# First MLP of a fused attention kernel: an order written by hand in place of a planned one

## The chip, the cores and the metric

The kernel runs on one core of a Trainium2 chip. The metric is the device time of one execution in microseconds (us). The engines are named as in the profile: PE (TensorE, matrix products and transposes), PEld (its weight loads), DVE (VectorE), ACT (ScalarE), POOL (GpSimd) and SP (SyncE, which here issues the DMAs). Each engine works off its own queue in order and waits at an instruction until its operands and its target are ready.

## What is computed

Attention over 4 batches of 8 heads, then two MLPs over 2304 tokens. The change is in the first MLP, `_moe_ref`, and in the preparation of the weights of the second, which runs beside it.

```python
def _moe_ref(x, w_in, w_out, g_ln):          # x 2304x512, w_in 512x1024, w_out 1024x512
    h = x @ w_in
    e = np.exp(h - np.max(h, axis=-1, keepdims=True))
    sm = e / (np.sum(e, axis=-1, keepdims=True) + 1e-09)
    solu = h * sm
    mu = np.mean(solu, axis=-1, keepdims=True)
    var = np.mean((solu - mu) ** 2, axis=-1, keepdims=True)
    return ((solu - mu) / np.sqrt(var + 1e-06) * g_ln) @ w_out

def _moe2_ref(x, w_gate, w_val, w_out):      # d_ff 1536
    gate = 1.0 / (1.0 + np.exp(-(x @ w_gate)))
    return gate * (x @ w_val) @ w_out
```

The weights arrive as 64-bit floats. Every product is computed from two parts of each operand, a high part and the rest (`hi`, `lo`), with three products hi·lo, hi·hi, lo·hi.

## The kernel before

The first MLP (class `Moe1`, from L606) works on 18 blocks of 128 tokens, t = 0 to 17. For one block:

- `xsplit` (L648) splits the attention's result X into `xs` hi (ACT, L653; DVE at L655 for the first three) and lo (POOL for blocks 2 to 5, otherwise DVE; L656). There are two `xs` buffers.
- `hidden` (L658): 24 matmuls of 512 columns (L674) into a PSUM tile `h` of 128x1024 (two buffers), then the statistics: the maximum (DVE, L682), the exponential with its sum (ACT, L690), reciprocal and product (DVE, L695 to L699), the square with its sum (ACT, L702, written to a bf16 scrap tile `sq` in SBUF), three small operations on POOL (L703 to L706, the power of -1/2 among them) and the normalisation (ACT, L707).
- `lntrans` (L717): 8 transposes on PE (L730) into two PSUM tiles `pl`, then `hilo` (L146): hi on ACT (L147), lo on DVE (L148), into `lnT`, which holds three blocks (a group) and has two buffers.
- `proj` (L748): for each group of three blocks 4 x 24 matmuls of 384 columns (L740) into PSUM tiles `po` (two buffers), copied back to X by ACT (L746).

The 18 blocks thus issue 432 matmuls for h, 144 transposes and 576 matmuls for po.

Beside it run two conversions of weights from 64-bit floats. `w_out` (L623) makes w_out's six chunks 2 to 7 (`rawwo`, `exwo`, `wo`): one load of 512 KB, then DVE (L108, L111, L121, L130), ACT (L118, L137, L642) and POOL (L641, L154). `Moe2.convert` (L827) makes each of the first six of twelve chunks of the second MLP's weights in 15 steps and 6 trailing steps that fall beside the next chunk's: three loads of 512 KB, 12 operations on DVE, POOL's products (L861) and sums (L875), hi on ACT (L883), lo (L889) and stores to DRAM (`scrg`, `scro`; L895, L896, L908, L909). In the first MLP all lo parts lie on POOL (`eng = nc.gpsimd`) and the tile `M` has one buffer; `lo_o` writes in place into `ex`, which is stored from there.

The order: the attention (`A.run(hooks)`, L1204) stands in a `manual_schedule`, in which each engine issues its instructions as the program writes them; blocks 0 and 1 of h and the statistics of block 0 are hooked into it. Everything of `Moe1` after that, with `A.last_conversions()` and the statistics of block 1 (`b1(a1())`, L1206, L1207), stands outside, and a planner places it; `steps` (L773) gives the planner its priorities, `merge` (L48) mixes the conversion steps in, and `issue_after` keeps conversion steps behind the last block's maximum on DVE. In `steps` a block's transposes stand one block behind its matmuls. The planner may place an instruction between those of a manual section where its operands allow it.

After the first MLP, `diffs` and `parts` (L952, L967) split X for the second MLP, and `m2.run` (L1117) works that off in a manual section; it is not changed, except that it uses `convert` for the other six chunks.

Of the kernel before, what the change touches and what calls it, by code (L numbers as in the profile page):

```python
# [32 lines left out]
def f32(ap):  # L33
    return ap.bitcast(F32)
# [13 lines left out]
def kernel(  # L48
# [21 lines left out]
    P = 128  # L70
# [92 lines left out]
    class Attention:  # L163
        def __init__(self, sb, ps, xe):
# [11 lines left out]
            self.small = sb.tile([P, 32], F32, tag="first", name="first")  # L176
            at = 7 * NFIRST
            self.rs = [self.small[:, at + 9 * n : at + 9 * n + 9] for n in range(2)]
# [26 lines left out]
            self.sum = [sb.tile([P, 9, 2], F32, tag=f"sum{n}", name=f"sum{n}") for n in range(2)]  # L205
# [12 lines left out]
        def gates(self):  # L218
# [8 lines left out]
            self.o9 = sb.tile([P, HP, 9], F32, tag="o9", name="o9")  # L227
# [366 lines left out]
        def last_conversions(self):  # L594
            for nm in "arbphl":
                for x in EXTRA[NP + 1]:
                    getattr(self, f"cv_{nm}")(x, self.pr[x])
# [5 lines left out]
    LAG = 7  # L603
    NFIRST = 2

    class Moe1:  # L606
        def __init__(self, xe, wi):
            self.xe, self.wi = xe, wi
            self.lnT, self.ln, self.xs, self.last, self.lasts = {}, {}, {}, None, []
            self.lt = self.sb = self.ps = self.spare = None  # L610

        def queue(self, steps):


            def one(f):
                if self.last is None:
                    return f()
                with tc.issue_after(self.last):
                    f()

            return [lambda f=f: one(f) for f in steps]

        def w_out(self, wp, stage, gl):  # L623

            self.wo = list(wo)
            for c in range(len(wo), NF1):
                self.wo.append(
                    [wp.tile([P, DM], F32R, tag=f"wo{x}{c}", name=f"wo{x}{c}") for x in "hl"]
                )

            def one(c):
                raw, ex, m = staged(stage, f"wo{c}")
                load_raw(raw, moe_w_out[c * P : c * P + P, :].unsqueeze(1))
                f64_a(raw, ex[:, 0], ex[:, 1])
                f64_r(ex[:, 0])
                scale_out(ex[:, 1], c)
                f64_b(raw, ex[:, 0], ex[:, 1], gl16[:, c : c + 1])
                hi, lo = self.wo[c]
                halves = [slice(256 * h, 256 * h + 256) for h in range(2)]
                for sl in halves:  # L640
# [637 lines left out]
```

## Time and profile before

| | us |
|---|---|
| median of 3 runs | 860.56 (860.41 to 862.53) |
| the profiled execution | 863.18 |
| its span, first to last instruction | 861.4 |
| attention alone on PE, to the first matmul of block 2 | 0 to 222.3 |
| first MLP after that, to the first matmul of the second | 222.3 to 441.0 |
| second MLP | 441.0 to 861.4 |

Over the span PE is busy 97%, DVE 73%, ACT 58%, POOL 58%. The profiled execution is 2.6 us above the median. The profile's busy time of PE counts matmuls that overlap in its pipeline; the pace of a row of matmuls is read from the time between the start of the first and the start of what follows, as the chain of waits shows it.

### The profile page before, as it was taken

The page shows a single profiled execution, that of the slowest core. Times are in us where ns is not written, and L with a number is a line of the kernel's source. Part 1 is how long each engine was busy: PE and PEld are TensorE (multiplying, and loading weights), DVE is VectorE, ACT ScalarE, POOL GpSimd, SP SyncE. Part 2 cuts the span into 40 slices and gives each one's busy share as a digit, 9 for nine tenths or more (in the row PEclk, how much of TensorE's full clock was granted, in tenths as well). Part 3 has the DMA queues.
Part 4 walks back from the last instruction along what each step waited for, and adds up shares of the span by engine and source line. Part 5 has one row for each costly group of instructions (what it writes and reads, how often), then busy time and mean ns, then how long its engine had stood idle before and what let it go on. Part 6 is the DMA issues. An engine that isn't in the chain of part 4 may idle for free.

```text
span 861.4 us, 15033 instructions
## 1 busy us (share of the span) xinstructions
PE 838.3 (97%) x5020; PEld 732.6 (85%) x5020; DVE 631.5 (73%) x1394; ACT 502.1 (58%) x1089; POOL 502.4 (58%) x631
## 2 busy tenths in 40 slices
PE   7999999999989999999999999999999999999998
PEld 5777777777778897888998999899899999999996
DVE  6899999997899777873427778788876445846645
ACT  5899999997888766775523446445533223423221
POOL 5777778775478978986105746776556242432111
PEclk9899999999999999999999999999999999999999
DMA  6443445330224655552059857993898863391662
GB/s 147 112 103 91 109 99 120 89 82 26 80 80 147 205 186 163 180 172 73 25 211 355 264 197 240 397 363 111 298 405 300 273 212 114 96 382 48 236 240 98
DMA packets 134140, 153.56 MB, mean 178 GB/s; under 512 B 67376, under 2 KB 101424, under 8 KB 134064
## 3 DMA queue, kind: packets, MB, share of 16 engines
q1 hardware_dynamic: 134064, 152.61, 54.7%
q8 instruction: 40, 0.66, 0.3%
q14 instruction: 36, 0.29, 0.1%
HBM read 116.40 MB, written 36.18 MB: 177 GB/s over the span
## 4 chain that ended last, share of the span: by engine, by line
PE 68%; POOL 10%; DVE 10%; DMA 6%; issue 2%; ACT 2%; SPq 1%; DVEq 0%; POOLq 0%; ACTq 0%
PE acc L1079 15%; PE s L1026 15%; PE g L1026 7%; PE x L500 5%; PE po L740 5%; PE sc L391 4%; PE v L1026 4%; POOL M L889 4%; PE h L674 2%; PE x L485 2%; DMA scro<-ex 2%; POOL M L861 1%; PE sc L382 1%; POOL M L875 1%; DMA gv0v<-scrg 1%
## 5 line engine op out<-in xcount | busy, mean ns | idle before, releaser
L1079 PE MATMUL acc<-o,G 128*128 128x512 f32 x648 | 181.6, 390 | 0.2 <-DVE G L1045 0.2
L1064 POOL TENSOR_TENSOR vl<-vl,sg 128x384 f32<-128x384 f32 x36 | 37.1, 1031 | 212.8 <-ACT sg L1063 212.8
L1079 PEld LDWEIGHTS acc<-o,G 128*128 128x128 f32 x648 | 118.5, 188 | 10.3 <-DVE G L1045 0.7
L430 POOL TENSOR_SCALAR p<-p,first,o 128x256 f32<-128x256 f32 (+3 forms) x142 | 92.0, 663 | 5.0 <-ACT ex L118 1.9
L674 PE MATMUL h<-wih,xs 128*128 128x512 f32 x288 | 83.7, 400 | 2.5 <-DVE e L699 1.4
L419 ACT ACTIVATE p<-p,nm 128x128 f32<-128x128 f32 (+2 forms) x144 | 82.7, 583 | 0.7 <-DVE nm L413 0.6
L1056 ACT ACTIVATE sg<-sg 128x384 f32<-128x384 f32 x36 | 18.9, 525 | 94.4 <-DVE sg L1055 94.4
L740 PE MATMUL po<-lnT,woh 128*128 128x384 f32 x288 | 73.7, 336 | 0.0
L1045 DVE TENSOR_TENSOR G<-vl,G 128x384 fp32r<-128x384 f32 x72 | 54.1, 751 | 20.5 <-ACT G L1042 20.3
L674 PEld LDWEIGHTS h<-wih,xs 128*128 128x128 f32 x288 | 52.9, 188 | 14.6 <-ACT xs L653 2.0
L1042 ACT CAST G<-vl 128x384 fp32r<-128x384 f32 x72 | 37.1, 515 | 42.5 <-POOL vl L1064 33.9
L1063 ACT ACTIVATE sg<-sg 128x384 f32<-128x384 f32 x36 | 18.9, 526 | 70.5 <-DVE sg L1062 70.4
L1050 DVE TENSOR_TENSOR u<-s,p 128x384 f32<-128x384 f32 x36 | 20.0, 556 | 54.3 <-PE s L1026 52.8
L413 DVE CUSTOM_DVE_ANT_0 p<-sc,mask 128x128 f32<-128x128 f32 (+3 forms) x128 | 54.6, 479 | 1.4 <-PE sc L391 1.2
L861 POOL TENSOR_TENSOR M<-ex 128x256 f32<-128x256 f32 x48 | 41.4, 884 | 23.7 <-DVE ex L130 20.4
L889 POOL TENSOR_TENSOR M<-M,hi 128x256 fp32r<-128x256 f32 x60 | 54.2, 926 | 0.2
L740 PEld LDWEIGHTS po<-lnT,woh 128*128 128x128 f32 x288 | 52.4, 189 | 0.1
L740 PE MATMUL po<-lnT,wol 128*128 128x384 f32 x144 | 48.5, 336 | 0.0
L118 ACT ACTIVATE ex<-ex,consts 128x512 int32<-128x512 int32 (+1 forms) x56 | 36.2, 647 | 20.4 <-DVE ex L108 18.8
L338 POOL TENSOR_TENSOR G<-E,zm 128x640 f32<-128x640 f32 x16 | 24.9, 1556 | 36.4 <-DVE E L335 31.7
L674 PE MATMUL h<-wil,xs 128*128 128x512 f32 x144 | 45.5, 395 | 0.0
L121 DVE SCALAR_TENSOR_TENSOR ex<-raw,ex 128x512 int32<-128x512 int32 (+1 forms) x56 | 43.1, 770 | 2.4 <-ACT ex L118 2.3
(711 smaller groups left out, 2494.8 us busy)
## 6 DMA issues: line engine op xcount, KB each, us to landing
o<-scro SPq DMA_DIRECT2D x36, 512.0 KB, 4.4
scrg<-hi SPq DMA_DIRECT2D x36, 256.0 KB, 4.8
scrg<-M SPq DMA_DIRECT2D x36, 256.0 KB, 4.4
raw<-in_moe_w_val_dram SPq DMA_DIRECT2D x12, 512.0 KB, 5.4
raw<-in_moe_w_gate_dram SPq DMA_DIRECT2D x12, 512.0 KB, 5.5
raw<-in_moe_w_out_dram SPq DMA_DIRECT2D x12, 512.0 KB, 4.8
out_dram<-X SPq DMA_DIRECT2D x18, 256.0 KB, 2.0
qt<-in_q_dram SPq DMA_DIRECT2D x32, 128.0 KB, 2.7
```

Of the source, the lines that this page charges most:

```text
L121: nc.vector.scalar_tensor_tensor(ex, raw[:, :, 1], -0x80000000, ex, ALU.bitwise_and, ALU.bitwise_or)
L413: nc.vector.tensor_tensor_reduce(p, x, m, -1.0, 3.0e38, ALU.add, ALU.min, nm)
L419: nc.scalar.activation(p, p, AF.Exp, bias=nm, scale=-1.0, accum_out=self.sum[n % 2][:, c, 0:1])
L430: eng.tensor_scalar(p, p, r["rs"][:, c : c + 1], og, ALU.mult, ALU.mult)
L500: nc.tensor.matmul(r["x", g][64 * hh : 64 * hh + 64, c0 : c0 + src.shape[1]], r["vt"][:, c : c + D], src, start=False, stop=j == 0,)
L674: nc.tensor.matmul(ph[:, j * 512 : j * 512 + 512], xs[:, s, c], self.wi[c][w][:, j * 512 : j * 512 + 512], start=(c == 0 and s == 0 and w ...
L740: nc.tensor.matmul(po, w[:, m * P : m * P + P], L[x][c // 4][:, c % 4], start=(c == 0 and n == 0), stop=(c == NF1 - 1 and n == 2),)
L861: nc.gpsimd.tensor_mul(out[:, sl], m[:, sl], e[:, sl])
L889: eng.tensor_sub(dst[:, sl].bitcast(F32R), dst[:, sl], f32(hi[:, sl]))
L1026: nc.tensor.matmul(po, W[:, a, c * P : c * P + P], xb[b][:, c], start=c + i == 0, stop=c == 1 and i == 2)
L1045: nc.vector.tensor_sub(G[:, 1, hs[h]], vl[:, h], f32(G[:, 0, hs[h]]))
L1079: nc.tensor.matmul(po, G[:, x, sl], o[:, w], start=first and i == 0, stop=stop and i == 2)
```

## The change

`Moe1` is rewritten so that the whole first MLP stands in manual sections; the arithmetic of the blocks is the same. In words:

- `run` issues per block t = 2 to 17: three conversion steps, half of the matmuls of h(t), the transposes of block t-2, the other half; then ACT's hi of t-2, the normalisation of t-1, the maximum and exponential of t, two conversion steps, DVE's lo of t-2, the hi of `xsplit(t+2)`, the product of t, the lo of `xsplit(t+2)`, the square of t, and `pieces(t)`, a third of a group's projection, with one conversion step behind each half of 12 matmuls and the rest at the end. Block 8 does all of h first and then finishes group 0.
- The chunks of w_out are converted one per block, in five steps; the second MLP's conversion starts at block 8 with 16 steps and has all of its steps issued by block 16.
- `square` writes into the PSUM tile `h` instead of a scrap tile in SBUF. The second column of the sum tile is set once instead of in every block (L689).
- `conversion` is called with `nc.vector, 2`: two of five lo parts of a chunk go from POOL to DVE, and `M` has two buffers. `ho` holds both parts, `lo_o` writes there and not into `ex`, and one store of 512 KB takes the place of two of 256 KB.
- The statistics of block 1 and the last conversions of w_out's chunks 0 and 1 move into the attention's manual section, behind it; `run` and `last` (the tail, mixed with `diffs` and `parts`) are two manual sections of their own.
- The unused tile `odd` ahead of w_in grows from 24 to 56 words, so the tiles of w_in lie 128 bytes further. `sum` and `o9` share one tile; the columns for the statistics lie in `consts`.

```diff
+        def square(self, t, first=None):
+            e, va, su = self.ln[t], self.small(t, "va", first), self.st[t, "su"]
+            sq = self.ph[t] if first is None else first.spare
+            nc.scalar.activation(sq, e, AF.Square, bias=su, scale=-1.0 * F1, accum_out=va)
...
+        def parts(self, t, n):
...
+                if n == 0:
+                    nc.scalar.copy(hi, self.pl[t, h])
+                else:
+                    nc.vector.tensor_sub(lo, self.pl[t, h], f32(hi))
...
+        def run(self, wp, stage, conv):
...
+            outs = {c: self.w_out(c, wp, stage) for c in range(2, NF1)}
+            later, done = [], 0
+            for c in (2, 3):
+                outs[c][0]()
+            outs[2][1]()
+            for n in range(2):
+                self.xsplit(NFIRST + 1, n)
...
+            for t in range(NFIRST, NBLK):
+                if t >= NF1:
+                    n = min(len(conv), 16 + (len(conv) - 16) * (t - NF1) // (NBLK - NF1 - 2))
+                    later += conv[done:n]
+                    done = n
+                go(3)
+                mms = [f for c in range(NC) for f in self.h(t, c)]
+                at = len(mms) if t == NF1 else len(mms) // 2
+                for f in mms[:at]:
+                    f()
+                if t == NF1:
+                    outs[t - 1][4]()
+                    for f, copy in self.pieces(0):
+                        f(), copy and copy()
+                for x in range(2):
+                    self.trans(t - 2, x)
+                for f in mms[at:]:
+                    f()
+                self.parts(t - 2, 0)
+                if t > NFIRST:
+                    self.norm(t - 1)
+                self.max(t)
+                if NFIRST < t < NF1:
+                    outs[t - 1][4]()
+                self.exp(t)
+                go(2)
+                self.parts(t - 2, 1)
+                if t + 2 < NBLK:
+                    self.xsplit(t + 2, 0)
+                if t < NF1:
+                    outs[t][2]()
+                self.mul(t)
+                if t + 2 < NBLK:
+                    self.xsplit(t + 2, 1)
+                self.square(t)
+                if t < NF1:
+                    outs[t][3]()
+                    if t + 2 < NF1:
+                        outs[t + 2][0]()
+                    if t + 1 < NF1:
+                        outs[t + 1][1]()
+                for f, copy in self.pieces(t):
+                    f(), copy and copy()
+                    go(1)
+                go(len(later))
+
+        def pieces(self, t):
+
+            if t == 0:
+                return [
+                    (lambda m=m: self.product(0, m, [6, 7]), lambda m=m: self.result(0, m)) for m in range(2)
+                ] + self.halves(0)[4:]
+            if t < NF1:
+                cs = {5: list(range(4)), 6: [4], 7: [5]}.get(t)
+                return [(lambda m=m: self.product(0, m, cs), None) for m in range(2)] if cs else []
+            g, i = divmod(t - 5, GB)
+            return self.halves(g)[3 * i : 3 * i + 3]
...
             def save_o():
-                nc.sync.dma_start(d[1][:, 0, 0], f32(st["ho"]))
-                nc.sync.dma_start(d[1][:, 0, 1], f32(st["e", "o"][:, 1]))
+                nc.sync.dma_start(d[1][:, 0], f32(st["ho"]))
...
-    odd.tile([P, 24], F32, tag="odd", name="odd")
+    odd.tile([P, 56], F32, tag="odd", name="odd")
...
         with tc.manual_schedule():
             A.run(hooks)
-        A.last_conversions()
-        b1(a1())
+            for f in (m1.max, m1.exp, m1.mul, m1.square):
+                f(1, A)
+            A.last_conversions("ar")
+            m1.norm(1)
+            A.last_conversions("bphl")
...
+            first, conv = m2.conversion(range(EARLY), cv, nc.vector, 2)
+            with tc.manual_schedule():
+                m1.run(wp, cv, [lambda: [x() for x in first], *conv])
...
-        merge(steps[n1:], m2.diffs(0, tp) + m2.parts(0, xp))
+        with tc.manual_schedule():
+            merge(m1.last(), m2.diffs(0, tp) + m2.parts(0, xp))
```

## Rows read from the trace of the kernel before

**Rows 1.** Busy time by stretch: us, each engine's busy (count), clock, DMA.
```profile
222.30:276.70 54.40, 49.72 (x242) 41.89 (x240) 51.48 (x91) 46.75 (x80) 40.78 (x62) 0.97 0.31 101
276.70:391.00 114.30, 110.69 (x579) 98.75 (x579) 87.24 (x133) 81.62 (x143) 99.05 (x142) 1.00 0.56 181
```

**Rows 2.** Chain that ended last, 395 to 470: start us, us, what.
```profile
400.53 5.57 PE h L674 x24
...
419.49 0.87 PE pl L730 x8
420.36 20.80 PE po L740 x120
...
455.26 0.68 PE acc L1079 x3
```

**Rows 3.** Waits of PE, 222.3 to 441: us in total, times, longest.
```profile
PE pl L730 <- ACT e L707: 3.6, 3, 1.8
PE pl L730 <- DVE lnT L148: 3.1, 3, 2.3
PE h L674 <- DVE e L699: 1.4, 2, 0.9
PE h L674 <- ACT lnT L147: 1.0, 1, 1.0
```

**Rows 4.** Busy time by stretch, right behind a wait of PE of 2.3 us.
```profile
251.76:255.40 3.64, 3.64 (x14) 3.64 (x14) 3.39 (x7) 2.93 (x7) 3.60 (x6) 0.53 0.34 129
```

**Rows 5.** ACT in order of time: exponential, square, normalisation of one block.
```profile
251.16 1.13 ACT L690 ACTIVATE e<-h,hm 128x1024 f32<-128x1024 f32 x1
...
254.19 1.15 ACT L702 ACTIVATE sq<-e,su 128x1024 bf16<-128x1024 f32 x1 [0.68 <-DVE e L699]
...
257.91 1.24 ACT L707 ACTIVATE e<-e,su,rd 128x1024 f32<-128x1024 f32 x1
```

**Rows 6.** Line L705, whole span: count, ns min/median/max, first and last start.
```profile
L705 POOL TENSOR_TENSOR rd<-va,consts x16: 547/552/1143, 241.7 to 415.0; 128x1 f32<-128x1 f32 x16
```

**Rows 7.** Instructions in order of time around 219 to 227: DVE, then ACT.
```profile
219.51 1.22 DVE L682 TENSOR_REDUCE first<-h 128x1 f32<-128x1024 f32 x1
...
224.27 0.48 DVE L144 COPY X<-x 128x320 f32<-128x320 f32 x1
...
219.31 0.60 ACT L653 CAST xs<-X 128x512 fp32r<-128x512 f32 x1
```

**Rows 8.** Groups of DVE, 270 to 390: busy us, mean ns, idle before.
```profile
L130 DVE SCALAR_TENSOR_TENSOR ex<-raw,ex 128x512 f32<-128x512 uint16 x17 | 16.5, 972 | 0.4 <-ACT ex L847 0.4
L121 DVE SCALAR_TENSOR_TENSOR ex<-raw,ex 128x512 int32<-128x512 int32 x17 | 14.9, 878 | 2.3 <-ACT ex L118 2.3
L699 DVE SCALAR_TENSOR_TENSOR e<-h,rs,e 128x1024 f32<-128x1024 f32 x10 | 12.8, 1280 | 0.2
L111 DVE TENSOR_SCALAR ex<-raw 128x512 int32<-128x512 int32 x16 | 12.7, 792 | 0.0
L148 DVE TENSOR_TENSOR lnT<-pl,lnT 128x512 fp32r<-128x512 f32 x19 | 12.3, 679 | 3.6 <-ACT lnT L147 3.6
L682 DVE TENSOR_REDUCE hm<-h 128x1 f32<-128x1024 f32 x10 | 12.1, 1212 | 2.6 <-PE h L674 2.6
L656 DVE TENSOR_TENSOR xs<-X,xs 128x512 fp32r<-128x512 f32 x10 | 9.3, 928 | 0.6 <-ACT xs L653 0.6
L108 DVE TENSOR_SCALAR ex<-raw 128x512 int32<-128x512 int32 x16 | 9.1, 569 | 16.4 <-POOL su L706 4.9 <-POOL M L861 4.4 <-DMA scro<-ex 3.7
```

**Rows 9.** Line L889 (lo parts), whole span: count, ns min/median/max.
```profile
L889 POOL TENSOR_TENSOR M<-M,hi x60: 728/915/1205, 274.9 to 662.8; 128x256 fp32r<-128x256 f32 x60
...
L889 DVE TENSOR_TENSOR M<-M,hi x12: 677/982/1514, 477.4 to 664.4; 128x512 fp32r<-128x512 f32 x12
```

**Rows 10.** DMA issues of SP: the first loads of two chunks in a row.
```profile
314.38 0.38 SPq L105 DMA_DIRECT2D raw<-in_moe_w_val_dram  x1
...
335.54 0.38 SPq L105 DMA_DIRECT2D raw<-in_moe_w_val_dram  x1
```

More of the change, by code (lines that the diff above doesn't have):

```diff
@@ L608, in __init__ @@
             self.xe, self.wi = xe, wi
[L609 to L639, printed above, removed]
+            self.lnT, self.ln, self.xs, self.ph, self.st, self.po, self.pl = ({} for _ in range(7))
@@ new lines, in __init__, with w_out, load, one @@
+            self.lt = self.ps = None
+        def w_out(self, c, wp, stage):
+            st = {}
+            halves = [slice(256 * h, 256 * h + 256) for h in range(2)]
+            def load():
+                st["raw"] = stage.tile([P, 512, 2], I32, tag="raw", name=f"rawwo{c}", bufs=2)
+                load_raw(st["raw"], moe_w_out[c * P : c * P + P, :].unsqueeze(1))
+            def one():
+                st["ex"] = ex = stage.tile([P, 2, 512], I32, tag="ex", name=f"exwo{c}", bufs=2)
+                f64_a(st["raw"], ex[:, 0], ex[:, 1])
+            def two():
+                f64_r(st["ex"][:, 0])
+                scale_out(st["ex"][:, 1], c)
+            def three():
+                f64_b(st["raw"], st["ex"][:, 0], st["ex"][:, 1], gl16[:, c : c + 1])
+                e, m = (f32(st["ex"][:, i]) for i in range(2))
@@ L644, in one, with xsplit @@
                     pool_lo(lo[:, sl], m[:, sl], hi[:, sl])
-            return [lambda c=c: one(c) for c in range(len(wo), NF1)]
-        def xsplit(self, t, hi_eng=None):
-            xs = self.xs[t] = self.xe.tile([P, 2, NC, P], F32R, tag="xs", name=f"xs{t}")
-            hi, lo = (xs[:, i].rearrange("p c (n t) -> p n c t", t=64) for i in range(2))
+            return load, one, two, three, four
+        def xsplit(self, t, n, first=None):
+            if n == 0:
+                self.xs[t] = self.xe.tile([P, 2, NC, P], F32R, tag="xs", name=f"xs{t}")
+            hi, lo = (self.xs[t][:, i].rearrange("p c (n t) -> p n c t", t=64) for i in range(2))
@@ new lines, in last, with piece, tr @@
+        def last(self):
+            n, g = NBLK, NBLK // GB
+            assert (n - 1 - 5) % GB == 0 and (n - 1 - 5) // GB == g - 2
+            def piece(x):
+                f, copy = x
+                return [f] + ([copy] if copy is not None else [])
+            def tr(t):
+                return [lambda: [self.trans(t, x) for x in range(2)], lambda: [self.parts(t, x) for x in range(2)]]
+            p, q = self.halves(g - 2)[3:], self.halves(g - 1)
+            out = piece(p[0]) + piece(p[1]) + tr(n - 2) + [lambda: self.norm(n - 1)] + piece(p[2]) + piece(p[3])
+            out += tr(n - 1) + piece(p[4])
+            return out + [f for x in q for f in piece(x)]
@@ L1192, with h, one @@
         m1 = Moe1(xe, wi)
-        (g0, a0, b0), (g1, a1, b1) = (m1.hidden(t, A) for t in range(NFIRST))
         def split(t):
-            return lambda: m1.xsplit(t, nc.vector)
-        sums = []
+            return lambda: [m1.xsplit(t, n, A) for n in range(2)]
+        def h(t):
+            steps = []
+            def one(i):
+                if i % 6 == 0:
+                    steps[:] = m1.h(t, i // 6, A)
+                for f in steps[i % 6 : i % 6 + 2]:
+                    f()
+            return [lambda i=i: one(i) for i in range(0, 6 * NC, 2)]
+        g0, g1 = h(0), h(1)
         hooks = {
```

234 lines of the change are left out of this document (99 added, 135 removed).

## The prediction

> **What bounds the kernel now.** I read the busy times by stretch first, then the chain of waits around the end of the first MLP, then PE's waits there. In the two stretches of the first MLP PE is busy 49.72 of 54.40 and 110.69 of 114.30 us [rows 1]; the reader is to see that DVE (51.48 of 54.40) is as full in the first and POOL (99.05) nearly so in the second. The chain gives PE's pace where nothing is late: 24 matmuls of h in 5.57 us, eight transposes in 0.87, 120 matmuls of po in 20.80 (0.173 each) [rows 2]. Between the first matmul of block 2 (222.3) and that of the second MLP (441.0) PE has 16 x 5.57 + 18 x 0.87 + 576 x 0.1733 = 89.1 + 15.7 + 99.8 = 204.6 us to do, in 218.7 us. Nothing that the change does to the first MLP can win more than the 14.1 us between. Of these PE's waits with a releaser are 3.6 + 3.1 + 1.4 + 1.0 = 9.1 [rows 3], nearly all of them at or around the transposes, which stand only one block behind their matmuls. Behind one wait of 2.3 us stands a stretch of 3.64 us with a granted clock of 0.53, that is between 1.2 and 2.4 GHz but near the lower [rows 4]; it did work of about half its length, so 1.7 us were lost there. The rest, 14.1 - 9.1 - 1.7 = 3.3, I put down to joints too small to be named (18 sets of transposes, each a change from matmul to transpose and back); I let them stay.
>
> So the forecast is a new sum for the slack: what PE will wait in blocks 2 to 7, in blocks 8 to 17, and the 3.3.
>
> **Blocks 2 to 7: a chain through ACT, DVE and POOL.** Transposes two blocks behind take the old waits away (most of the 9.1), and leave what is slower than PE over several blocks. In the new order ACT does normalisation(t-1), exponential(t), square(t), and then must have the three small POOL operations before normalisation(t). Before, from an exponential's start to the square's took 254.19 - 251.16 = 3.03, from there to the normalisation 257.91 - 254.19 = 3.72, and that 1.24: 8.0 us a block [rows 5]. POOL's power took from 0.55 to 1.14 us [rows 6], median 0.55; POOL is emptier here after the change, so I take 7.6, with 7.0 and 8.0 as ends. PE needs 5.57 + 0.87 = 6.44 a block.
> Where it starts: the maximum of block 1 stood at 219.51, ahead of DVE's last copies of the attention; now it is issued behind them (the one at 224.27 [rows 7], which moves up about 1 us when the maximum's 1.22 leave the queue). Put at 223.5, the maximum, 3.03, 3.72 and 1.24 end at 232.7. PE comes to transposes(1) in the middle of h(3), at 222.3 + 5.57 + 0.87 + 2.79 = 231.5: a wait of 1.2. Each later block's normalisation ends 7.6 later, at 240.3 and 247.9, and PE comes 6.44 after its last: 1.2 and 1.2 more. From block 5 on a piece of group 0 (24 matmuls, 4.16 us) gives PE other work and the chain is ahead. Sum 3.6. The two PSUM buffers of h give the same: h(4) needs square(2), which ends at 232.7 + 3.03 + 1.15 + 0.2, within the wait already counted. The lower end is 0.5 (7.0 a block, maximum at 223.0), the upper 6.8 (rival B).
>
> **Blocks 8 to 17: DVE.** From block 9 to 16 PE's work a block is 5.57 + 0.87 + 5.55 (32 matmuls of po on average) = 12.0. Beside it go 81 conversion steps in eight blocks, 10.1 a block or 0.675 of a chunk's 15. A chunk costs DVE 3 x (0.569 + 0.792 + 0.878 + 0.972 = 3.21) [rows 8] and now two lo parts more: 0.677 to 1.514, median 0.982 [rows 9], so 9.63 + 1.96 = 11.6; times 0.675 is 7.8. The block's own: maximum 1.21, two lo parts 1.36, product 1.28, split 0.93 [rows 8], small ones 0.3: 5.1. Together 12.9 against 12.0, an excess of 0.9 x 8 = 7.2 us by the end. A late DVE reaches PE through `pl` (the lo parts of t-2 set it free) and `h` (the product). From the end of h(t-1) to transposes(t-2) PE has a piece and half of h, 5.55 + 2.8 = 8.3, and DVE must do the maximum, two lo parts and two steps there, 1.21 + 1.36 + 1.54 = 4.1: cover of 4.2 us. Excess less cover is 3.0; nothing is left if the conversion runs at the shorter of its durations. I take 2.0, with ends 0 and 7.2.
>
> **What relieves.** 24 lo parts of 0.915 (two of five, in six chunks) leave POOL, 22 us, and 12 of twice the width come to DVE (in the 12.9). The 16.4 us that DVE stood before L108, among them 4.4 for POOL's `M` and 3.7 for the store of `ex` [rows 8], lose those two reasons: `M` has a second buffer and the store reads `ho`. They are no direct gain, for PE did not wait there.
>
> **Edits that I cost at nothing.** The square's target in PSUM: 1.15 us into SBUF beside 1.13 for the exponential that reads PSUM and 1.24 for the normalisation [rows 5]. No row has a write of this size from ACT to PSUM; by those neighbours it is -0.1 to +0.1 on ACT, inside the 7.6. It holds `h` 1.3 us longer than the product did, counted above; without that cover it would be 0.7 on each of three blocks. SP: one store for two, and loads of w_out two blocks ahead, take entries off a queue that nobody in the path waits for; memset gone from 16 blocks, off POOL's chain. The tail mixes the same work by hand; PE from 420.36 to the end of po is one row without a break [rows 2], so only a wait of the first matmul of the second MLP could cost there, 0 to 0.5. w_in's address: h's matmuls take 5.57 / 24 = 0.232, those of the second MLP 0.68 / 3 = 0.227 for the same 512 columns [rows 2]. If the address were the reason, 432 x 0.005 = 2.2 us would be won, and as much could be lost at the new one; no row shows an effect of an address, so 0.
>
> **Sum.** New slack 3.6 + 2.0 + 3.3 = 8.9 against 14.1: 5.2 us less. The profiled execution (863.18, span 861.4) would be 858.0; it lies 2.6 above the median of the runs, so the median goes from 860.56 to 855.4.
>
> **Rivals.**
> A is the forecast, 855.4.
> B, the order is kept too strictly. Before, the planner put the split of block 3 at 219.31 and a maximum at 219.51 among the attention's last instructions [rows 7]. If the new section's first steps stay behind the last conversions and normalisation(1) (232.7), block 3's split is ready at 233.9 instead of in time for 222.3 + 5.57 + 0.87 = 228.8: PE stands 5.1 us and loses 1.7 to the clock as in [rows 4], 6.8 in place of 3.6. Time 858.6. Against it: the same two rows show that operands, not text, decide across that border. Chance 0.10.
> C, slower: DVE becomes the bound. Before, in 10 blocks it also stood 16.4 + 2.3 + 0.4 = 19.1 us for other engines inside its conversions [rows 8], 1.9 a block. If a fixed order keeps these stops (a step waits at the head of DVE's queue, and maximum, lo parts and product of the block wait behind it), a block takes 12.9 + 1.9 = 14.8: 8 x 2.8 - 4.2 = 18.2 in place of 2.0, time 871.6. It makes the kernel slower from about 13.5 us a block on (8 x 1.5 - 4.2 = 7.8). Against it: two of the three named reasons go, and the steps are spread with a piece of PE's work between. Chance 0.13.
> D, almost all goes: chain 7.0 (0.5) and no stall of DVE. Slack 3.8, gain 10.3, time 850.3; with the w_in term up to 2.2 less. For it: with lo parts at their shortest (0.677) DVE's block is 12.5, and 8 x 0.5 = 4.0 lies within the cover of 4.2. Chance 0.20.
> E, DVE's and POOL's conversion work stand in each other's way. The same lo part took DVE 0.677 to 1.514 and POOL 0.728 to 1.205 [rows 9], so something stretches them. If DVE's operations with two operands in SBUF and POOL's could not run together at all, a block would hold 0.675 x (3 x (0.878 + 0.972) + 2 x 0.982) = 5.1 on DVE, 0.93 for its split and 0.675 x 15 x 0.728 = 7.4 on POOL (six products, four sums and five lo parts of a chunk, at the shortest), 13.4 in place of 12.0: 8 x 1.4 - 4.2 = 7.0 of stall in place of 2.0, time 860.4. For it: the old mix counted so (19 operations on POOL, none of the lo parts on DVE, 21.2 / 12 splits) makes 5.55 + 13.8 + 1.6 = 21.0, and from one chunk's first load to the next's were 21.2 us [rows 10]. Against it: the sum of 12.9 already holds durations that are stretched, and the same 21.2 is also just PE's pace. Chance 0.07.
> The Trainium skill has such a rule ("SBUF — State Buffer", section "Who interferes with whom"): a VectorE instruction with two SBUF inputs contends with a GpSimd instruction that reads SBUF, whoever issues first holding the shared pair for its whole instruction. The trace agrees in the spread of [rows 9]; that the exclusion is complete no row here shows; by the rule alone the time would be that of E.
>
> **How the numbers follow.** A 0.50, D 0.20, C 0.13, B 0.10, E 0.07. 0.3% (2.6 us) is about what a measurement of this kernel can tell from no change. A lies in that bound on its slow side with 0.05 of its 0.50. Faster: 0.45 + 0.20, and 0.01 of B, 0.66; same: 0.05 of A, 0.07 of B, 0.06 of E, 0.18; slower: C with 0.02 of B and 0.01 of E, 0.16. The range takes in A's ends, D with most of the w_in term, B and E, and leaves out most of C: 848.5 to 863.5.
>
> **What would show it.** Right: in the profile after, PE's waits at `pl` for normalisation and lo part together under 3 us; normalisations of blocks 2 to 4 some 7.6 us apart; block 1's maximum near 223.5; DVE's work in blocks 9 to 16 near 12.9 us a block, with waits for `M` and the store gone; the square at 1.15 us still; h at 5.57. Wrong: a wait of PE above 3 us before h(3) (B), a wait at `pl` that grows from block 9 to 16 (C, E), conversion operations that are longer than before (E), h's 24 matmuls shorter or longer than 5.57 (w_in), or the first matmul of the second MLP waiting.

## The result, and the profile after

The changed kernel took 872.50 us (median of 4 runs, 871.49 to 873.57) against 861.49 for the kernel before on the same chip: ratio 1.0128, 95% interval 1.0107 to 1.0150. It is 11.0 us slower; 855.4 was forecast. The profiled execution took 873.04 us, its span is 871.2.

Where the time went is read from the same stretch as before. The first matmul of block 2 starts at 222.2 as it did, the first of the second MLP at 453.3 (before: 441.0). So the first MLP lost 12.4 us, and the second MLP, 420.4 us long before by the span, is now 417.9: it gave 2.5 back. The waits of PE in the first MLP, after (us in total, times, longest), which answer to [rows 3]:

```profile
PE pl L712 <- DVE lnT L722: 7.6, 6, 2.1
PE po L731 <- ACT woh L640: 3.7, 1, 3.7
PE pl L712 <- DVE e L689: 3.5, 1, 3.5
PE pl L712 <- ACT hi L928: 1.4, 1, 1.4
PE h L665 <- ACT h L694: 0.9, 1, 0.9
PE pl L712 <- ACT e L683: 0.6, 1, 0.6
```

They sum to 17.7 us, nearly twice the 9.1 of before. Where they stand is seen in PE's instructions in order of time (start, duration, what, idle before it and its releaser); shown are six of the seven waits above 1 us, five in front of transposes and one in front of a projection (the seventh, 1.39 at 414.39, is that for ACT's `hi` above):

```profile
228.72 1.63 PE L712 MATMUL pl<-ident,e 128*128 128x128 f32 x8 [3.47 <-DVE e L689]
...
238.58 1.23 PE L712 MATMUL pl<-ident,e 128*128 128x128 f32 x8 [1.70 <-DVE lnT L722]
...
285.26 1.01 PE L731 MATMUL po<-lnT,woh 128*128 128x384 f32 x2 [3.69 <-ACT woh L640]
...
333.96 1.41 PE L712 MATMUL pl<-ident,e 128*128 128x128 f32 x8 [2.08 <-DVE lnT L722]
...
374.18 1.23 PE L712 MATMUL pl<-ident,e 128*128 128x128 f32 x8 [1.35 <-DVE lnT L722]
...
402.07 1.23 PE L712 MATMUL pl<-ident,e 128*128 128x128 f32 x8 [1.32 <-DVE lnT L722]
```

Behind three of them PE ran at a lower clock, as it did once before [rows 4]. Busy time by stretch, after (the number behind POOL's count is the granted clock):

```profile
228.72:233.06 4.34, 4.34 (x16) 3.74 (x17) 2.91 (x8) 4.20 (x8) 2.57 (x5) 0.61 0.01 2
285.26:290.40 5.14, 5.14 (x16) 4.84 (x17) 0.00 (x0) 0.96 (x2) 1.41 (x2) 0.50 0.32 102
333.96:338.45 4.49, 4.49 (x17) 3.60 (x18) 3.78 (x9) 4.11 (x10) 1.44 (x4) 0.62 0.71 226
```

Against the pace of the same instructions elsewhere these stretches lost about 1.6, 2.5 and 1.8 us. PE's own work is now 16 x 5.48 + 15.7 + 99.8 = 203.2 us (24 matmuls of h take 5.48 where they stand in one row). So the 231.1 us from 222.2 to 453.3 are 203.2 of work, 17.7 of waits, 5.9 of low clock and 4.3 of small joints. In three places:

| | waits | low clock | sum | forecast |
|---|---|---|---|---|
| blocks 2 to 7 | 3.5 + 1.7 + 0.9 | 1.6 | 7.7 | 3.6 |
| block 8 | 3.7 | 2.5 | 6.2 | 0 |
| blocks 9 to 17 | 7.6 - 1.7 + 1.4 + 0.6 | 1.8 | 9.7 | 2.0 |
| joints | | | 4.3 | 3.3 |

**Blocks 2 to 7.** DVE in order of time, after:

```profile
224.40 1.22 DVE L678 TENSOR_REDUCE first<-h 128x1 f32<-128x1024 f32 x1
...
227.28 1.28 DVE L689 SCALAR_TENSOR_TENSOR e<-h,first,e 128x1024 f32<-128x1024 f32 x1
...
233.82 0.43 DVE L557 TENSOR_TENSOR wo<-ex,wo 128x256 fp32r<-128x256 f32 x1 [0.19 <-ACT wo L553]
235.94 0.43 DVE L108 TENSOR_SCALAR exwo<-rawwo 128x512 int32<-128x512 int32 x1 [1.70 <-DMA rawwo<-in_moe_w_out_dram]
236.29 0.42 DVE L111 TENSOR_SCALAR exwo<-rawwo 128x512 int32<-128x512 int32 x1
236.62 1.22 DVE L678 TENSOR_REDUCE consts<-h 128x1 f32<-128x1024 f32 x1
237.76 1.28 DVE L722 TENSOR_TENSOR lnT<-pl,lnT 128x512 fp32r<-128x512 f32 x2
```

Block 1's maximum starts at 224.40 (219.51 before [rows 7]). Its product ends at 228.6, and by the releaser that is what the transposes of block 0 wait for; as they do not read that product, I take it that their PSUM comes free with it. The attention's last conversions stand behind that product, then w_out's first conversion, which waits 1.70 us for its load, and only then block 2's maximum, at 236.62, though h(2) had ended near 234 and, without PE's wait, would have ended near 228.6. Block 1's own normalisation ends at 232.8 (ACT, after), and no transposes of blocks 2 to 7 wait for it or for a later one:

```profile
231.58 1.24 ACT L702 ACTIVATE e<-e,first 128x1024 f32<-128x1024 f32 x1
```

SP issues the load 12 us later than before (before, then after):

```profile
220.40 30.45 SPq L105 DMA_DIRECT2D rawwo<-in_moe_w_out_dram  x6
```
```profile
232.56 25.86 SPq L105 DMA_DIRECT2D rawwo<-in_moe_w_out_dram  x5
```

**Block 8.** The last chunk of w_out is the last thing of a chain that runs through ACT, DVE and POOL from block 2 on. The chain of waits, after, shows its pace at the exponentials:

```profile
245.67 1.10 ACT e L683 x2
...
253.37 1.11 ACT e L683 x2
...
261.22 1.10 ACT e L683 x2
...
282.68 1.89 POOL exwo L635 x2
284.59 0.63 ACT woh L640
285.26 12.64 PE po L731 x57
```

7.7 to 7.85 us a block, and group 0's projection needs that chunk at 281.6.

**Blocks 9 to 17.** DVE first stands idle in block 8, then has no time to spare. Two instructions of DVE in block 8 and the costliest groups of DVE from 304.85 to 410.08, blocks 9 to 16 (busy us, mean ns of one, idle before and its releasers):

```profile
283.89 1.21 DVE L130 SCALAR_TENSOR_TENSOR ex<-raw,ex 128x512 f32<-128x512 uint16 x1
298.98 1.29 DVE L722 TENSOR_TENSOR lnT<-pl,lnT 128x512 fp32r<-128x512 f32 x2 [13.88 <-ACT lnT L720]
```
```profile
L121 DVE SCALAR_TENSOR_TENSOR ex<-raw,ex 128x512 int32<-128x512 int32 x17 | 16.6, 974 | 6.7 <-ACT ex L118 6.7
L130 DVE SCALAR_TENSOR_TENSOR ex<-raw,ex 128x512 f32<-128x512 uint16 x16 | 15.2, 947 | 2.5 <-ACT ex L892 2.5
L111 DVE TENSOR_SCALAR ex<-raw 128x512 int32<-128x512 int32 x16 | 11.6, 725 | 0.0
L108 DVE TENSOR_SCALAR ex<-raw 128x512 int32<-128x512 int32 x16 | 10.6, 662 | 3.0 <-DMA raw<-in_moe_w_out_dram 1.7 <-POOL M L906 1.3
L934 DVE TENSOR_TENSOR M<-M,hi 128x512 fp32r<-128x512 f32 x10 | 10.1, 1011 | 2.6 <-POOL M L920 2.6
```

DVE's busy time in this stretch is 90.2 us and its stops 6.7 + 2.5 + 3.0 + 2.6 = 14.8: 105.0 of 105.2 us. But the stretch is cut by PE's blocks, and DVE is behind them: its maximum of block 9 starts at 316.78, 5.5 us after the end of h(9) at 311.23, so that the stretch holds seven blocks' maxima and products beside the conversions of eight. The expectations below reckon with 11.3 + 1.85 = 13.1 us a block from it. By DVE's own count, from that maximum to the one of block 16 at 410.56 (us, DVE's busy time and count, clock, DMA):

```profile
316.78:410.56 93.78, 82.20 (x123) 0.98 0.60 194
```

That is 13.4 us a block, 11.7 busy and 1.7 of stops. PE, with 94.5 us of work in the eight, takes 11.8. Before, the planner had issued the second MLP's first load at 258.20; now it is issued at 273.77 (SP's issues, before and after):

```profile
258.20 0.38 SPq L105 DMA_DIRECT2D raw<-in_moe_w_val_dram  x1
```
```profile
273.77 0.38 SPq L105 DMA_DIRECT2D raw<-in_moe_w_val_dram  x1
```

From 222.2 to 304 DVE is busy 53.11 us, where it was 73.75 before: 20.6 us of conversion that had been done by then were still to do.

### The profile page after: what moved, and what is told of

The parts are those of the page before. It is cut to its first block, busy times and chain, and to the rows that moved or that the text cites. A ratio compares the mean times of both kernels' runs of the same rounds, so it can differ in the third digit from the quotient of the medians.

```text
span 871.2 us, 14952 instructions
## 1 busy us (share of the span) xinstructions
PE 839.7 (96%) x5020; PEld 734.0 (84%) x5020; DVE 640.4 (74%) x1406; ACT 501.5 (58%) x1089; POOL 483.4 (55%) x592
## 4 chain that ended last, share of the span: by engine, by line
PE 72%; DVE 11%; ACT 7%; POOL 4%; issue 3%; DMA 2%; SPq 0%; POOLq 0%; DVEq 0%; ACTq 0%
PE s L1073 16%; PE acc L1126 16%; PE g L1073 8%; PE po L731 5%; PE x L503 5%; PE sc L394 4%; PE v L1073 4%; PE x L488 2%; ACT h L694 2%; PE sc L385 2%; ACT e L683 1%; DVE ex L130 1%; DVE ex L121 1%; DVE M L934 1%; POOL exwo L635 1%
## 5 line engine op out<-in xcount | busy, mean ns | idle before, releaser
L433 POOL TENSOR_SCALAR p<-p,first,cols 128x256 f32<-128x256 f32 (+3 forms) x142 | 92.0, 662 | 5.2 <-ACT ex L118 1.9
L665 PE MATMUL h<-wih,xs 128*128 128x512 f32 x288 | 86.9, 406 | 0.9 <-ACT h L694 0.9
L118 ACT ACTIVATE ex<-ex,consts 128x512 int32<-128x512 int32 (+1 forms) x56 | 36.2, 646 | 32.2 <-DVE ex L108 32.2
L906 POOL TENSOR_TENSOR M<-ex 128x256 f32<-128x256 f32 x48 | 41.0, 873 | 13.5 <-DVE ex L130 13.5
L920 POOL TENSOR_TENSOR M<-M 128x256 f32<-128x256 f32 x48 | 45.5, 958 | 1.1
```

Source lines behind the costliest of these rows:

```text
L433: eng.tensor_scalar(p, p, r["rs"][:, c : c + 1], og, ALU.mult, ALU.mult)
L665: lambda s=s, w=w, j=j: nc.tensor.matmul(ph[:, j * 512 : j * 512 + 512], xs[:, s, c], self.wi[c][w][:, j * 512 : j * 512 + 512], start=(c ...
L906: nc.gpsimd.tensor_mul(out[:, sl], m[:, sl], e[:, sl])
L920: ops[i][0](*ops[i][1:])
```

## The experiments

Theory: three separate losses, each a place where the written order puts something behind a wait that the planner had put elsewhere (block 2's maximum on DVE, w_out's last chunk in block 8, DVE's conversions after block 8). Rivals: POOL or the address of w_in sets the time, or one loss simply takes over what another gives back. All ratios are to the kernel before on the same chip. It took 860.9 to 862.2 us in these sets of runs, so that the times of two edited kernels from different sets can be compared to about 1 us.

**w_in back at its old address.**

```diff
-    odd.tile([P, 56], F32, tag="odd", name="odd")
+    odd.tile([P, 24], F32, tag="odd", name="odd")
```

> The changed kernel with the unused tile at its old 24 words, so w_in at its old address. Address theory: 24 matmuls of h go back from 5.48 us (0.2283 each, read in the trace of after) to 5.57 (0.232), 432 x 0.004 = 1.6 to 1.8 us more: 874.2. Rival, the pace of h comes from the order of the work and not from the address: 872.5 within 0.6, and h stays at 5.48.

Measured 872.41 us, ratio 1.0126 (1.0108 to 1.0144): no difference in time. But the matmuls did change. Matmuls of line 665 by form, 56 words (two rows) and 24 words (count, ns min/median/max):

```profile
L665 PE MATMUL h<-wih,xs x288: 387/390/776, 205.1 to 418.0; 128*128 128x512 f32 x144
L665 PE MATMUL h<-wil,xs x144: 387/389/628, 205.6 to 417.5; 128*128 128x512 f32 x144
```
```profile
L665 PE MATMUL h<-wih,xs x288: 387/396/774, 204.0 to 416.1; 128*128 128x512 f32 x144
L665 PE MATMUL h<-wil,xs x144: 390/392/629, 204.6 to 415.6; 128*128 128x512 f32 x144
```

Block 8's 24 matmuls took 5.48 us with 56 words (275.40 to 280.88) and 5.60 with 24 (274.63 to 280.23). The theory holds for the pace and the rival for the time. Where the 1.9 us went is not shown: PE's waits in the first MLP sum to 17.4 us here and to 17.7 in the changed kernel, and this profiled execution has two stretches at a low clock where that of the changed kernel has three.

**The lo parts of the conversion back on POOL.**

```diff
-            first, conv = m2.conversion(range(EARLY), cv, nc.vector, 2)
+            first, conv = m2.conversion(range(EARLY), cv, nc.gpsimd, 2)
```

> The changed kernel with all lo parts of the conversion on POOL, as before. Theory: in blocks 9 to 16 DVE is full, 11.3 us of work and 1.85 us of stops inside the conversion per block against some 12.0 of PE. Without 0.675 x 2 x 1.01 = 1.4 us of lo parts it needs 11.7, and the late waits of PE (7.9 us, and 1.8 at a low clock) go for the most part: 863 to 866. Rival: POOL, 10.3 us a block, takes over the 2.0 to 2.4 and is then the late one: 870 to 874, with PE waiting for the same transposes and DVE for POOL.

Measured 871.52 us, ratio 1.0115 (1.0100 to 1.0130). Busy time by stretch (PE, PEld, DVE, ACT, POOL), 304 to 410, of this kernel and then of the changed one:

```profile
304.00:410.00 106.00, 98.85 (x519) 87.39 (x518) 86.34 (x123) 73.34 (x129) 97.15 (x125) 1.00 0.59 186
```
```profile
304.00:410.00 106.00, 99.50 (x514) 87.70 (x513) 90.76 (x133) 72.77 (x128) 82.88 (x104) 0.98 0.58 186
```

DVE is 4.4 us emptier, POOL 14.3 fuller, and PE now waits at its transposes for normalisations (3.6 us) beside the lo parts (2.6). Those normalisations stand on ACT behind a high part of the conversion (L947), which waits 2.05 to 2.25 us each time for POOL's product (L906). The rival holds: the lo parts on DVE are not what made the kernel slow, and elsewhere they would cost as much.

**Transposes of block 0 behind all of h(2).**

```diff
-                at = len(mms) if t == NF1 else len(mms) // 2
+                at = len(mms) if t in (NFIRST, NF1) else len(mms) // 2
```

> The changed kernel with the transposes of block 0 behind all of h(2) and not in its middle. Theory: the transposes wait for the PSUM that block 1's product on DVE frees at 228.6, since block 1's maximum now starts 5 us later; with 2.8 us more of h ahead of them the wait falls from 3.5 to under 1 and the low clock behind it (1.6 us) goes, and exponential(2) and all of ACT's chain to block 8 start earlier, so that the wait of 3.7 us for w_out's chunk 7 and its low clock (2.5) shrink too: 865 to 868.5. Rival: the wait only moves to the next transposes, which wait for the same chain: 871 to 873.

Measured 871.83 us, ratio 1.0119 (1.0104 to 1.0134). The first wait shrank to 0.78, and the next one took it over (PE in order of time):

```profile
238.20 1.97 PE L712 MATMUL pl<-ident,e 128*128 128x128 f32 x8 [6.03 <-DVE lnT L722]
```

The rival holds. Block 2's maximum on DVE still started at 236.33, and the lo part of block 0, which frees `pl`, stands behind it. The wait in front of the transposes was a symptom.

**A conversion step behind each part of group 0's projection.**

```diff
                     for f, copy in self.pieces(0):
                         f(), copy and copy()
+                        go(1)
```

> The changed kernel with one conversion step behind each of the six parts of group 0's projection in block 8. Theory: DVE stands 13.9 us in block 8, its lo parts of block 6 being at the head of its queue while PE works off group 0, and the six steps that it could have done there are what it is late by afterwards. Six steps of 1.0 to 1.2 us done there take 6 to 7 us from a backlog that costs 7.9 us of waits and 1.8 of low clock: 864 to 867. Rival: DVE is too slow in every block (13.1 against 12.0), and a head start helps only until it is used up, gain 2 to 4: 868.5 to 870.5; or another engine is late: 872.

Measured 866.97 us, ratio 1.0063 (1.0041 to 1.0085): 5.5 us faster than the changed kernel. Of the 7.9 us of waits from block 9 on 4.7 are left: 2.7 for lo parts on DVE, 2.0 for ACT. The theory holds: the larger part of the late loss came from the start of that stage. The 4.7 that are left fit the rival, a DVE that is slower than PE in every block.

**Block 1's statistics hooked into the attention.**

```diff
-                lambda: [f(0, A) for f in (m1.mul, m1.square)], lambda: m1.norm(0),
+                lambda: [f(0, A) for f in (m1.mul, m1.square)],
...
+            (NP, "cv_b"): [lambda: [f(1, A) for f in (m1.max, m1.exp)], lambda: m1.norm(0)],
+            (NP, "x0_c"): [lambda: [f(1, A) for f in (m1.mul, m1.square)]],
...
-            for f in (m1.max, m1.exp, m1.mul, m1.square):
-                f(1, A)
```

> The changed kernel with block 1's maximum, exponential, product and square hooked back among the attention's last steps, where the planner had put them in the kernel before (maximum at 219.5). Theory: the early loss is all one delay of 4.9 us, from the maximum (224.4 for 219.5) through the product (227.3 for 222.4) to everything behind it on DVE: the wait at the transposes of block 0 (3.5 and 1.6 of clock) and most of that at block 1's (1.7) go, and block 2's maximum, which stood at 236.6, comes 4 us earlier: 872.5 - 5 = 866.5 to 868.5. Rival: that wait is only moved, as the run with the transposes behind h(2) showed, because DVE still stands for the first load of w_out (landed at 235.9): 870.5 to 872.

Measured 871.40 us, ratio 1.0116 (1.0101 to 1.0132). The maximum of block 1 moved to 218.19, and nothing came of it: PE waited 6.53 us for block 0's lo part at 236.87. Block 2's maximum was still at 234.91, because the hooked square put POOL's small operations ahead of the attention's last products (DVE stood 3.73 us behind that), and because w_out's first conversion still waited for its load (1.97 us). The rival holds, with a second cause that I had made myself.

**One buffer for M.**

```diff
-            first, conv = m2.conversion(range(EARLY), cv, nc.vector, 2)
+            first, conv = m2.conversion(range(EARLY), cv, nc.vector, 1)
```

> The changed kernel with one buffer for M. The second buffer of 8 KB shifts the ring of raw tiles in SBUF: its first load waited for the last conversion of the attention's weights (issued 232.56, before the change 220.40) and DVE stood 1.7 us for it at the head of its queue, block 2's maximum behind it. Theory: the load is issued near 220 again, that stop goes, maximum of block 2 at about 235 for 236.6, gain 1 to 2 early; against it DVE and POOL stand for M in the late blocks, where DVE is full, 0.675 x 1 to 2 us a block, up to 5 lost: 870 to 876. If M's second buffer is worth nothing (rival): 870.5 to 871.5.

Measured 891.41 us, ratio 1.0348 (1.0333 to 1.0363), beyond both expectations. The early half of the theory holds: with 8 KB less the ring of raw tiles lies elsewhere, and the load is issued as early as before the change. Block 2's maximum starts at 234.90, and the wait of 1.70 in front of the transposes of block 1 is gone. (SP's issues; below it POOL's waits from 295 to 430:)

```profile
220.33 36.37 SPq L105 DMA_DIRECT2D rawwo<-in_moe_w_out_dram  x5
```
```profile
POOL M L906 <- DMA scrg<-M: 28.5, 4, 8.1
```

The late half was sized far too small. POOL's products wait 28.5 us in four places for the store of `M`, and in a written order all of POOL's queue, the statistics' small operations among it, stands behind them. The second buffer is worth some 19 us in this order, and its price is 12 us of delay of one load.

**ACT's high part of a w_out chunk behind the exponential.**

```diff
                 self.max(t)
+                self.exp(t)
                 if NFIRST < t < NF1:
                     outs[t - 1][4]()
-                self.exp(t)
```

> The changed kernel with ACT's high part of a w_out chunk behind the block's exponential and not ahead of it. Theory: from block 2 to 8 ACT, DVE and POOL run in a cycle of 7.8 us a block (chain of waits: exponentials at 245.7, 253.4, 261.2, 269.1, 276.9) with that high part in it, which stands for POOL's products; without it the cycle is some 7.0, the chain arrives at block 8 up to 4 us earlier and the wait of 3.7 us there and its clock (2.5) shrink: 867.5 to 870. Rival: the cycle goes through the normalisation anyway (it ends 0.1 before the high part starts), nothing is won: 872.

Measured 871.77 us, ratio 1.0123 (1.0105 to 1.0141). The wait in block 8 went from 3.7 to 3.0 and no more. The rival holds for the time. Its reason fits the trace of after, where a normalisation ends 0.1 us before the high part starts, but no run took the normalisation out of the cycle.

**Hook, fill and ACT's order together.**

> The three edits together: block 1's statistics hooked into the attention's end, a conversion step behind each part of group 0's projection in block 8, and ACT's high part behind the exponential. If the losses are separate (early delay 5, head start of DVE 5.5 as measured, block 8's wait 2 to 4): 858 to 861, at or below the kernel before. If the late stage takes back what the early one gives, since DVE is full there whatever comes before: 865 to 867.

Measured 867.33 us, ratio 1.0065 (1.0043 to 1.0086), no better than the fill alone. It looks like the second expectation, but the trace gives another reason: the early wait is there as in the run with the hooks alone (6.28 us at 236.96), so nothing early had been given that could be taken back.

**Both causes of the early delay.** The square hooked behind POOL's last products, and w_out's chunk 2 behind block 2's square:

```diff
+            (NP, "cv_b"): [lambda: [f(1, A) for f in (m1.max, m1.exp)], lambda: m1.norm(0)],
+            (NP, "x0_c"): [lambda: m1.mul(1, A)],
+            (NP, "cv_h"): [lambda: m1.square(1, A)],
...
-            outs[2][1]()
...
-                if t < NF1:
+                if NFIRST < t < NF1:
                     outs[t][2]()
...
                 self.square(t)
+                if t == NFIRST:
+                    outs[t][1](), outs[t][2]()
...
```

> Both causes of the early delay taken away at once: block 1's maximum, exponential and product hooked into the attention's end with the square behind the last products of POOL there, and the first conversion of w_out's chunk 2 (which stood on DVE for a load that lands at 231 to 236) behind block 2's square. Theory: the wait that only moved so far (3.5 at block 0's transposes, 6.0 or 6.5 at block 1's) is one delay of block 2's maximum on DVE (236.6, 235.0 in the run with the hooks, 229.5 before the change) by work queued ahead of it. It then stands at 229 to 231, and the early waits with their low clock (3.5 + 1.7 + 0.9 + 1.6 = 7.7) go but for 1 to 2: 866 to 868. Rival: block 8 takes it back, w_out's chunk 7 being bound by the 7.8 us cycle: its wait grows from 3.7 to 8 or more, total 870 to 872.

Measured 865.71 us, ratio 1.0046 (1.0031 to 1.0062): 6.8 us faster than the changed kernel. DVE, from its instructions in order of time:

```profile
228.18 1.22 DVE L678 TENSOR_REDUCE consts<-h 128x1 f32<-128x1024 f32 x1
```

Block 2's maximum is at 228.18 (236.62 in the changed kernel). PE's early waits are one of 1.92 us, at 238.75, and block 8's is 3.64, no longer than it was. The theory holds.

**The same with the fill, two steps each, and ACT's order.**

> The same with two conversion steps behind each part of group 0's projection in block 8 and ACT's high part of a chunk behind the exponential. Theory: early delay and late backlog are separate, so their gains add: 872.5 - 5.5 (as one step behind each part gave) - 5 to 7 = 860 to 862, and the second step takes 1 to 3 more: 858 to 861. Rival, DVE is too slow in every late block whatever its start: 864 to 867.

Measured 859.83 us, ratio 0.9975 (0.9958 to 0.9991). The early gain and the late gain add up.

**Half of h(9) ahead of group 0's projection.**

```diff
                 if t == NF1:
+                    nxt = [f for c in range(NC) for f in self.h(t + 1, c)]
+                    for f in nxt[: len(nxt) // 2]:
+                        f()
                     outs[t - 1][4]()
...
```

> The kernel of the run before, and half of h(9) moved ahead of group 0's projection in block 8. Theory: PE stands there for w_out's chunk 7 (2.9 to 3.7 us) and then runs at a low clock (2.5 lost); 12 matmuls of h are 2.74 us of work that needs nothing from that chunk, so the wait falls under 1 us and the low clock goes: 4 to 5 us faster than the run before. Rival: the cycle of statistics in blocks 2 to 8 is later by as much as PE is earlier, so that the wait is larger than before and half of it stays: 1 to 2.5 us.

Measured 856.71 us, ratio 0.9945 (0.9927 to 0.9964), 3.1 below the run before it. PE's waits in the first MLP and at the start of the second:

```profile
PE pl L712 <- DVE lnT L722: 4.6, 3, 1.9
PE pl L712 <- ACT e L683: 2.2, 2, 1.6
PE g L1081 <- DVE u L1105: 0.4, 1, 0.4
PE po L731 <- ACT woh L640: 0.2, 1, 0.2
PE po L731 <- POOL wol L154: 0.2, 1, 0.2
```

Block 8's wait is 0.2, as the theory said, and the gain of 3.1 is between the two expectations. The low clock in block 8 is gone too (1.00 from 278.39 to 282.39), but this profiled execution has one behind the early wait of 1.92 (0.63 from 238.48 to 243.12, about 1.7 us lost), which that of the run before has not (1.00 behind the same wait). The first matmul of the second MLP stands at 435.9 (before 441.0, changed 453.3). This version is faster than both kernels.

**The fastest kernel with w_in at its old address.**

> The fastest kernel so far with the unused tile at 24 words again, so w_in at its old address. In the changed kernel the address made no difference to the time (872.41 with 24 words, 872.50 with 56), though block 8's 24 matmuls of h took 5.60 us for 5.48: PE waited for others and the 0.12 a block were taken out of its waits. Here PE waits 7 us in all in the first MLP, and most blocks have no wait. Theory: the 16 x 0.12 = 1.9 us now show, for the most part: 1.2 to 1.9 above the 856.7 of the run with 56 words, so 857.9 to 858.6, and h(8) takes 5.60. Rival: the remaining waits still absorb them: within 0.5 of 856.7.

Measured 856.18 us, ratio 0.9946 (0.9933 to 0.9960), an interval inside that with 56 words. The matmuls are slower as the theory said: the 36 of h in one row in block 8 take 8.40 us for 8.20, which is 5.60 for 24. The time does not show it, so the rival holds. That PE's waits absorb it is only half of what the two profiled executions show: the waits are 6.1 us for 7.2, and the early stretch at a low clock (1.7 us) is missing. Whether this is so in the other executions is not shown.

## Why the prediction was wrong

**The frame held.** PE's work in the first MLP is 203.2 us by the trace of after (204.6 forecast) and the second MLP, which was given no change, gave 2.5. What failed is the new slack: 27.9 us in place of 8.9, 19.0 too little. With 1.4 for the faster h and 2.5 for the second MLP, the 858.0 of the profiled execution become 858.0 + 19.0 - 1.4 - 2.5 = 873.1; it took 873.04.

**Blocks 2 to 7, the step that failed first (7.7 for 3.6).** The cycle (7.6 forecast, 7.7 to 7.85 seen), block 1's maximum (223.5 forecast, 224.40 seen) and the end of its normalisation (232.7 forecast, 232.8 seen) were near enough. What failed is the step from there to PE: none of the three waits of 1.2 for a normalisation came, and waits of 3.5, 1.7 and 0.9 for DVE's product of block 1, its lo part of block 0 and a square stood in their place. The start of block 2 was wrong: its exponential was put at 232.7, right behind that normalisation, and came at 237.87. I followed the late maximum along its own block only (exponential, square, normalisation) and asked when PE would want transposes(1). What stood behind it in DVE's queue I did not follow: the attention's last conversions, then w_out's chunk 2, then block 2's maximum; nor that the PSUM of the first `pl` comes free with block 1's product. The run with the transposes moved and the run with block 1's statistics hooked back only moved the wait (0.78 and then 6.03; 6.53); with the queue cleared it fell to 1.92 and 6.8 us came back. That settles this part.

**SP's loads, costed at nothing.** That its queue is one "that nobody in the path waits for" was wrong for the first load. It moved from 220.40 to 232.56, because `M`'s second buffer moved the ring into space that the attention's last conversion still used (SP waits there for DVE's L130, which ends at 232.5); one buffer put it back to 220.33. I had counted what a second buffer frees and not where it lies.

**Block 8, a missing term (6.2).** The forecast let the chain of statistics fall behind until block 5 and be caught up by group 0's pieces. It did, for the transposes. But w_out's chunks had been tied to the same chain, one a block, and the last one is wanted by the matmuls themselves. Giving PE 12 matmuls that do not need it took the wait to 0.2.

**Blocks 9 to 17, mis-sized (9.7 for 2.0).** The mechanism and the engine were named. The work of DVE was put at 12.9 us a block. The durations of its instructions do add up to 12.8, but an instruction starts some 0.08 us before the one ahead of it ends (235.94 + 0.43 against 236.29 in the rows above), and DVE is busy for 11.7. The stops inside the conversion, which were said to lose their reasons, stayed at 1.7 a block (1.9 before): the store went, of the waits for POOL's products 1.3 of 4.4 us were left and 2.6 for its sums came, and waits for ACT's L118 and L892 grew from 2.7 us in ten blocks to 9.2, since steps of one chunk now follow each other directly. So a block took DVE 13.4 us against PE's 11.8, an excess of 12.8 in eight blocks for the 7.2 forecast. The larger fault is the cover: 4.2 us were set against the excess, and DVE entered block 9 behind, after 13.88 us idle in block 8 with the lo part of block 6 at the head of its queue. The comparison that would have shown it needs no knowledge of the change beyond "starts at block 8": the kernel before had issued the second MLP's first load at 258.20. Filling those microseconds gave 5.5 us back and left 4.7 of waits. Two counts of PE's work were a little off and changed nothing: blocks 6 and 7 have 6 matmuls of group 0 each and not 24, and blocks 9 to 16 have 31.5 of po a block and not 32.

**What held.** The square into PSUM costs ACT nothing (1.12 us, 1.15 before) and delayed h once, by 0.9. The tail has no wait. POOL's relief was rightly given no gain: without it the time is the same (871.52 for 872.50), with POOL late in DVE's place. Without the second buffer of `M` the kernel would be 19 us slower still, though the prediction saw no direct gain in it. For w_in, 0 was right for the time, and the bound of 2.2 us for the work (16 x 0.09 = 1.4 by the two kernels' traces).

**The rivals.** C is the one that came closest, by its time (871.6) and by its mechanism. That its time is right is luck: its price was not what the late blocks cost (18.2 in its sum, 9.7 seen), for it added the stops to durations that overlap (14.8 us a block, 13.4 seen; 8 x 1.6 - 4.2 = 8.6), and its sign, a wait that grows from block 9 to 16, did not show (they lie between 0.5 and 2.1 without order). The rest of the loss stood in blocks 2 to 8. B as priced did not happen: h(3) had no wait for its split, though its sign, a wait above 3 us before h(3), did show. But its mechanism, first steps of the new section that stay behind the last conversions, is near to what happened to block 2's maximum, and its 6.8 to the 7.7 seen. For block 8 no rival had a loss. E's mechanism is in the trace. From 304 to 411 DVE did 17 instructions of L111; the eight with no POOL instruction beside them took 0.42 us each, the nine with POOL at work all through 0.95 to 0.97. One of each and a pair of POOL's beside the second (POOL is idle until 304.76):

```profile
304.25 0.42 DVE L111 TENSOR_SCALAR ex<-raw 128x512 int32<-128x512 int32 x1
...
314.75 0.96 DVE L111 TENSOR_SCALAR ex<-raw 128x512 int32<-128x512 int32 x1
...
314.51 1.80 POOL L906 TENSOR_TENSOR ex<-ex 128x256 f32<-128x256 f32 x2
```

Its price did not come on top, as the prediction had said against it: a conversion's four operations take 0.66 + 0.73 + 0.97 + 0.95 = 3.31 us on average, against the 3.21 of the forecast, so the stretch was in the 12.9 already. E's sum had left out L108 and L111, which are stretched too. No run took POOL away from beside DVE at an equal order.

**What stays open.** The 2.5 us that the second MLP gave: its largest wait went from 1.29 to 0.56 and two waits for loads of its weights, 0.9 together, are gone, which is more than half. No run was made on it.

## What to carry to other kernels

When a planned order is replaced by a written one, go through each engine's queue and ask, for every instruction that can wait (a load, another engine, a buffer), what the planner had let pass it; here a 1.7 us wait for a load and a few conversions stood between PE and a maximum that was ready. An idle engine ahead of a full stretch is part of that stretch's sum: compare how much of the side work was done by then before and after, not only the load per block. If undoing one cause only moves a wait, look for what the engine behind it has at the head of its queue before giving the theory up.

## What the runs showed of the hardware

- 128 bytes of shift in SBUF changed the matmuls that read w_in: median 390 and 389 ns at one address, 396 and 392 at the other, 5.48 against 5.60 us for a row of 24. It was no gain in time in either kernel (872.50 against 872.41, 856.71 against 856.18); what made up for it is shown in part only.
- In the changed kernel the granted clock fell behind PE's waits of 3.47 us (0.61), 3.69 (0.50) and 2.08 (0.62), between the levels of 1.2 and 2.4 GHz; behind those of 1.70, 1.35 and 1.32 us a stretch of 2 us shows 1.00. So each of the first three cost 1.6 to 2.5 us more than its length. Behind an equal early wait of 1.92 us the clock was 0.63 (over 4.64 us) in one of the edited kernels and 1.00 in the two runs before it.
- DVE's 128x512 conversions from SBUF to SBUF (L111) took 0.42 us with POOL idle and 0.96 with POOL at work on SBUF tiles beside them; its lo parts that read PSUM (L722) took 0.68 with POOL at work beside 12 of the 14.
- A larger tile in one ring delayed a load into another ring by 12 us, only by where the rings came to lie.
